# Zero products on TensorE in the waits of a fused Sinkhorn-attention and feed-forward kernel

## The chip, the cores and the metric

The kernel runs on one core of one Trainium2 chip. The metric is the device time of an execution in microseconds (us). The kernel before takes 242.38 us, the median of five runs that lie between 241.8 and 243.04.

TensorE (PE) multiplies matrices, VectorE (DVE) and ScalarE (ACT) do element-wise work and empty TensorE's accumulators in PSUM, GpSimd (POOL) issues most of the loads, and SyncE (SP) the stores and some small loads. Each engine works through its own list of instructions in order; semaphores make one wait for another.

## What is computed

Four batches of eight heads, 768 positions, head size 64. The positions are cut into 8 blocks of 96. A learned 8x8 matrix per head is normalised five times over rows and columns (Sinkhorn) and mixes the blocks of k and of v. Each block of q then attends to its own mixed block. The result, 3072 rows of 512, goes through a feed-forward layer of width 2048 with a squared ReLU.

```python
for _ in range(5):
    P = exp(P - max(P, axis=-1))
    P = P / (sum(P, axis=-1) + 1e-9);  P = P / (sum(P, axis=-2) + 1e-9)
k_sorted = einsum('bhij,bhjcd->bhicd', P, k_blocks)      # v_sorted in the same way
attn = softmax(q_block @ k_sorted_block.T / 8)           # block by block, 96 x 96
x = (attn @ v_sorted_block) as rows of 512
out = (s * relu(x @ w_in)**2 + b) @ w_out
```

## The kernel before

The work is cut into eight half-batches of 4 blocks x 96 = 384 rows, called t = 0 to 7 (t // 2 is the batch). One Python function emits each kind of piece, and the order in which the pieces are called is each engine's order of work; it is written out by hand from line 537 on. In the middle of the kernel `Queue` objects put attention pieces between feed-forward products. What the change touches lies before and in the first half-batch:

- `zt` (line 101) is a tile of zeros, and `warm_up(n)` (line 169) multiplies it by itself n times: 128x128 weights, 256 columns. Nothing reads the products.
- `q_half` (line 234) transposes half of q for batch 0; ScalarE copies the result to `qt`. Line numbers in the profile are those of the instruction: L244 for the transposes, L228 (VectorE) and L230 (ScalarE) for all copies out of PSUM, which go through `evac`.
- The Sinkhorn steps on `sn` (lines 187 to 201) alternate between ScalarE and VectorE.
- `build_pd1` calls `block_rows(0)`, whose product `pe` (L213) spreads the 8x8 matrices over 128 partitions; four VectorE instructions make the block matrix `pd1` from it (the last is L520).
- `k_piece` (L277) mixes the blocks of k with `pd1`, as product `tk`; the copies go to `ks`. `v_piece0` (L303) does it for v, 16 products of 64 columns per piece (`tv`), one copy each to `vs`. It reads its weights from `vb` with a stride of 64 elements.
- `s_piece` (L358) computes one pair of heads' scores for four blocks, and ScalarE takes their exp (L361, tile `at`).
- `p_piece` (L385) multiplies `at` by `vs` as `pv`. VectorE takes a reciprocal (L389) and writes the scaled values to `x` (L390). With `nn=2` it does only two of the four blocks, in one PSUM bank.
- `t_piece` (L413) transposes `x`; `ffn1` (L442) is the first feed-forward product, in eight slots of 8 products for two blocks or four.

Two pools of PSUM tiles matter. `psa` has three buffers of two banks (q transposes, the larger k pieces, v pieces, scores, feed-forward). `psb` has two buffers of one bank (zeros, `pe`, the smaller k pieces, the half-sized `p_piece` and `t_piece`). A tile can be taken again when everything that uses the earlier one in that buffer is done. In the kernel before, each zero product takes a new `psb` tile.

The loads that this part needs are issued on GpSimd's queue in this order: half of q, k and v of batch 0, the other half of q, then the weights, and later v, q and k of batch 1.

Of the kernel before, what the change touches and what calls it, by code (L numbers as in the profile page):

```python
# [9 lines left out]
FP = mybir.dt.float32  # L10
# [8 lines left out]
def kernel(  # L19
# [12 lines left out]
    nc = tc.nc  # L32
# [9 lines left out]
    HB = NB // 2  # L42
# [24 lines left out]
    psb = ctx.enter_context(tc.tile_pool(name="psb", bufs=2, space=bass.MemoryType.PSUM))  # L67
# [25 lines left out]
    def brows(b):  # L93
        return slice(b * 64, (b + 1) * 64), slice((b % 2) * 64, (b % 2) * 64 + 64)
# [6 lines left out]
    zt = const.tile([128, 256], BF)  # L101
# [41 lines left out]
    for c0 in range(0, d_ff, FCH):  # L143
        w = const.tile([128, NHP, FCH], BF, name=f"wi{c0}")
        nc.gpsimd.dma_start(
            out=w, in_=moe_w_in.rearrange("(hp p) f -> p hp f", p=128)[:, :, c0:c0 + FCH])
# [5 lines left out]
    for f0 in range(0, NF, FW):  # L152
        w = const.tile([128, FW, d_model], BF, name=f"wo{f0}")
        nc.gpsimd.dma_start(
            out=w, in_=moe_w_out.rearrange("(f p) n -> p f n", p=128)[:, f0:f0 + FW, :])
# [11 lines left out]
    ks = const.tile([128, 64, BLK], BF)  # L167

    def warm_up(n):
        for _ in range(n):  # L170
            wp = psb.tile([128, 256], FP, tag="b", name="wp")
            nc.tensor.matmul(out=wp, lhsT=zt[:, 0:128], rhs=zt, start=True, stop=True)  # L172

    def zero_pad(r0):
# [35 lines left out]
    def block_rows(g):  # L210

        pe = psb.tile([128, 512], FP, tag="b", name="pe")
        nc.tensor.matmul(out=pe[:, 0:NB * NB], lhsT=emat[:, g * 128:(g + 1) * 128],  # L213
                         rhs=sn.rearrange("p i j -> p (i j)"), start=True, stop=True)
        tmp = sk.tile([128, NB, NB], FP, name=f"tmp{g}")
        nc.vector.tensor_tensor(out=tmp, in0=pe[:, 0:NB * NB].rearrange("p (i j) -> p i j", j=NB),
                                in1=bcast(jsel, NB), op=ALU.mult)
        pt = sk.tile([128, NB], FP, name=f"pt{g}")
        nc.vector.tensor_reduce(out=pt, in_=tmp, axis=AX.X, op=ALU.add)
        return pt  # L220
# [5 lines left out]
    def evac(out, in_, eng):  # L226
        if eng == "v":
            nc.vector.tensor_copy(out=out, in_=in_)  # L228
        else:
            nc.scalar.copy(out=out, in_=in_)  # L230
# [3 lines left out]
    def q_half(half, eng):  # L234

        if half == 0:
            QT[0] = qtp.tile([128, NHP, S], BF, tag="qt", name="qt0")
        pr = slice(half * 64, half * 64 + 64)
        ps = psa.tile([128, 2, 1024], BF, tag="a", name="tq")
        for hp in range(NHP):  # L240
            for t in range(TQ):
                c0 = (hp % 2) * TG + t * 64
                for e in range(2):
                    nc.tensor.transpose(out=ps[e * 64:(e + 1) * 64, hp // 2, c0:c0 + 64],  # L244
                                        in_=qr[0][pr, 2 * hp + e, t, :], identity=ident[pr, pr])
        for a in range(2):
            evac(QT[0][:, 2 * a:2 * a + 2, half * TG:(half + 1) * TG].rearrange(
                     "q b (p t) -> q b p t", t=TQ),
                 ps[:, a, 0:2 * TG].rearrange("q (b t p) -> q b p t", b=2, t=TQ), eng)
# [15 lines left out]
    def k_piece(b, c0, nc2, nb, eng):  # L265

        pr = brows(b)[1] if nb == 1 else slice(0, 128)  # L270
        rhs = (pd1[pr] if b < 2 else pd2[pr, b - 2]).rearrange("p e m i -> p (e m i)")
        if nc2 * nb > 8:
            ps = psa.tile([128, nc2, nb * 64], FP, tag="a", name="tk")
        else:
            ps = psb.tile([128, nc2, nb * 64], FP, tag="b", name="tk")
        for c in range(nc2):
            nc.tensor.matmul(out=ps[:, c, :],  # L277
                             lhsT=kb[pr, c0 + 2 * c:c0 + 2 * c + 2, :].rearrange("p c d -> p (c d)"),
                             rhs=rhs, start=True, stop=True)
        g0 = (b % 2) * 32  # L280

        def half(cp):
            if b == 0:
                cs = slice(c0 + cp, c0 + 2 * nc2, 2)
            else:
                cs = slice(cp * (BLK // 2) + c0 // 2, cp * (BLK // 2) + c0 // 2 + nc2)
            for e in range(2):
                evac(ks[e * 64:(e + 1) * 64, g0:g0 + nb * 32, cs].rearrange(
                         "p (b g) c -> p b g c", b=nb),
                     ps[cp * 64:(cp + 1) * 64].rearrange(  # L290
                         "p c (b e g) -> p e b g c", b=nb, e=2)[:, e], eng)

        half(0)
        return lambda: half(1)

    def v_piece0(d0, n, eng):

        if n > 8:
            ps = psa.tile([128, n, 64], FP, tag="a", name="tv")
        else:  # L300
            ps = psb.tile([128, n, 64], FP, tag="b", name="tv")
        for t in range(n):
            nc.tensor.matmul(out=ps[:, t, :], lhsT=vb[0:64, :, d0 + t],  # L303
                             rhs=pd1[0:64].rearrange("p e m i -> p (e m i)"),
                             start=True, stop=True)
        evac(VS[0][:, :, d0:d0 + n], ps[0:BLK].rearrange("p t g -> p g t"), eng)
# [42 lines left out]
    def s_piece(t, hp):  # L349

        b, half = divmod(t, 2)
        g0 = (b % 2) * 32 + hp * NB + half * HB
        sc = psa.tile([BLK, 2, 512], FP, tag="a", name="sc")
        for n in range(HB):
            for e in range(2):
                pr = slice(e * 64, (e + 1) * 64)
                q0 = (half * HB + n) * BLK
                nc.tensor.matmul(out=sc[:, e, n * BLK:(n + 1) * BLK], lhsT=ks[pr, g0 + n, :],  # L358
                                 rhs=QT[b][pr, hp, q0:q0 + BLK], start=True, stop=True)
        at = atp.tile([BLK, 2, TG], BF, tag="at", name="at")  # L360
        nc.scalar.activation(out=at, in_=sc[:, :, 0:TG], func=AF.Exp, scale=scale)  # L361
        AT[t, hp] = at

    def p_piece(t, hp, n0=0, nn=HB):

        b, half = divmod(t, 2)
        at = AT[t, hp]
        if t not in X:
            X[t] = xp.tile([BLK, HB, d_model], BF, tag="x", name="x")
        x = X[t]  # L370
        atf = at.rearrange("p e t -> p (e t)")
        if nn < HB:
            p1 = psb.tile([128, 512], FP, tag="b", name="pv")
            pv = [p1[:, e * nn * VW:(e + 1) * nn * VW] for e in range(2)]
            pvv = p1[0:BLK, 0:2 * nn * VW].rearrange("p (e n w) -> p e n w", e=2, w=VW)
        else:
            p2 = psa.tile([128, 2, 512], FP, tag="a", name="pv")
            pv = [p2[:, 0], p2[:, 1]]
            pvv = p2[0:BLK, :, 0:nn * VW].rearrange("p e (n w) -> p e n w", w=VW)
        for e in range(2):  # L380
            for n in range(n0, n0 + nn):
                c0 = (e * HB + n) * BLK
                m = 128 if c0 + 128 <= 2 * TG else BLK
                gi = e * 32 + hp * NB + half * HB + n
                nc.tensor.matmul(out=pv[e][0:m, (n - n0) * VW:(n - n0 + 1) * VW],  # L385
                                 lhsT=atf[:, c0:c0 + m],
                                 rhs=VS[b][:, gi, :], start=True, stop=True)
        rec = rtp.tile([BLK, 2, HB], FP, tag="rec", name="rec")
        nc.vector.reciprocal(out=rec[:, :, 0:nn], in_=pvv[:, :, :, D])  # L389
        nc.vector.tensor_tensor(  # L390
            out=x[:, n0:n0 + nn, hp * 128:(hp + 1) * 128].rearrange("p n (e d) -> p e n d", e=2),
            in0=pvv[:, :, :, 0:D],
            in1=rec[:, :, 0:nn].unsqueeze(3).broadcast_to([BLK, 2, nn, D]), op=ALU.mult)
# [107 lines left out]
    def P2(t, hp):  # L501
        return lambda: (p_piece(t, hp), p_piece(t, hp + 1))
# [15 lines left out]
    def build_pd1():  # L518
        pt = block_rows(0)
        nc.vector.tensor_tensor(  # L520
            out=pd1, in0=hmask.rearrange("p (m e) i -> p e m i", e=2),
            in1=bass.AP(tensor=pt.tensor, offset=pt.offset,
                        ap=[list(pt.ap[0]), [0, 2], [0, NHP], list(pt.ap[1])]),
            op=ALU.mult)
# [10 lines left out]


    warm_up(38)
    q_half(0, "s")
    warm_up(12)
    build_pd1()  # L540
    k_piece(0, 0, 16, 1, "v")()
    k_piece(0, 32, 16, 1, "s")()
    k_piece(0, 64, 8, 1, "v")()
# [3 lines left out]
    v_piece0(32, 16, "v")  # L547
    s_piece(0, 0)
    s_piece(0, 1)
    v_piece0(48, 16, "v")  # L550
    s_piece(0, 2)
    s_piece(0, 3)
    q_half(1, "s")
    for hp in range(NHP):
        p_piece(0, hp, 0, 2)
    t_piece(0, "v", 0, 2)
    s_piece(1, 0)
    s_piece(1, 1)
# [4 lines left out]
    def P(t, hp, *r):  # L563
        return lambda: p_piece(t, hp, *r)
# [101 lines left out]
```

The softmax here doesn't subtract the row's maximum and nothing guards it: scores larger than these inputs give would overflow.

## Time and profile before

| what | value |
|---|---|
| median of five runs | 242.38 us (241.8 to 243.04) |
| profiled execution | 243.04 us |
| its span on the core | 241.3 us |
| mean granted clock of TensorE | 0.955 |
| PE busy in the span | 226.9 us, 94% |
| zero products (L172) | 50, 304 ns mean, 9.2 us busy |
| v products (L303) | 64, 271 ns mean, 6.0 us busy |

The profile is one execution, recorded by the hardware. Its span runs from the first to the last recorded instruction, and the execution took 1.74 us more than that. "Granted clock" is the share of full speed at which TensorE was let run. A product's duration contains its latency, and products overlap, so the distance between the starts of two of them is less than the duration. Each row names the line, the engine and the operation, with the output tile, an arrow and its inputs; "x16" means sixteen instructions merged into one row, and the brackets tell how long the engine stood idle before it and what ended that.

### The profile page before, as it was taken

The numbers are of one execution on the slowest core, as the hardware profiler recorded it, in microseconds if no ns is written. First come the engines' busy times: TensorE is split into PE (matmuls) and PEld (weight loads), VectorE is DVE, ScalarE is ACT, GpSimd is POOL, SyncE is SP. The second block draws the span as 40 slices with busy tenths as digits, with TensorE's granted clock in tenths as the row PEclk, the third lists the DMA queues.
The fourth block names the chain that finished last, engine by engine and source line by source line (L and its number), as shares of the span: only waits on it lengthen the run. The fifth ranks groups of instructions, "written<-read, shape, count | busy, mean of one in ns | idle before, by whom it ended". The sixth has DMA issues, their size and how long they took to land.

```text
span 241.3 us, 4882 instructions
## 1 busy us (share of the span) xinstructions
PE 226.9 (94%) x2059; PEld 135.9 (56%) x2080; DVE 134.1 (56%) x268; ACT 108.1 (45%) x154; POOL 39.4 (16%) x52
## 2 busy tenths in 40 slices
PE   8859799989999999999998999999999999999993
PEld 4558698855545555555554455666554556554441
DVE  5775547967993558766365748343353544342221
ACT  6356456435538541577726250656522225660000
POOL 7820000099960000460000000000000000000000
PEclk9975559999999999999999999999999999999999
DMA  4999999985999994599902061400014232001212
GB/s 59 183 196 211 220 200 206 229 211 95 136 158 173 273 307 104 117 114 105 161 11 87 3 152 46 109 0 3 1 47 125 69 109 47 0 3 43 79 51 87
DMA packets 29622, 27.33 MB, mean 113 GB/s; under 512 B 16928, under 2 KB 23840, under 8 KB 29088
## 3 DMA queue, kind: packets, MB, share of 16 engines
q0 software_dynamic: 8400, 15.21, 38.1%
q1 hardware_dynamic: 21200, 11.81, 20.8%
q8 instruction: 16, 0.26, 0.5%
q14 instruction: 6, 0.05, 0.1%
HBM read 29.63 MB, written 8.65 MB: 159 GB/s over the span
## 4 chain that ended last, share of the span: by engine, by line
PE 83%; DVE 7%; DMA 6%; issue 2%; POOL 1%; ACT 1%; POOLq 0%
PE hps L442 34%; PE ops L468 33%; DMA vb<-in_v_dram 6%; PE sc L358 3%; PE pv L385 3%; PE tv L303 2%; PE tk L277 2%; PE tq L259 2%; DVE x L390 2%; DVE ks L228 1%; PE tv L333 1%; DVE gt L447 1%; DVE vn L228 1%; DVE ot L459 1%; PE tq L244 1%
## 5 line engine op out<-in xcount | busy, mean ns | idle before, releaser
L442 PE MATMUL hps<-xt,wi 128*128 128x384 bf16 (+1 forms) x576 | 89.9, 314 | 1.0 <-DVE xt L228 1.0
L468 PE MATMUL ops<-wo,gt 128*128 128x512 bf16 x363 | 87.7, 379 | 1.5 <-issue 0.5
L446 ACT ACTIVATE rt<-hps 128x768 bf16<-128x768 f32 (+1 forms) x72 | 53.3, 740 | 53.8 <-PE hps L442 52.2
L442 PEld LDWEIGHTS <-wi 128*128 128x128 bf16 x576 | 54.7, 100 | 31.3 <-issue 2.3
L447 DVE TENSOR_TENSOR gt<-rt 128x768 bf16<-128x768 bf16 (+1 forms) x72 | 42.0, 586 | 42.3 <-ACT rt L446 41.8
L468 PEld LDWEIGHTS <-gt 128*128 128x128 bf16 x384 | 35.0, 98 | 38.4 <-issue 0.6
L361 ACT ACTIVATE at<-sc 96x768 bf16<-96x768 f32 x32 | 24.3, 802 | 35.2 <-PE sc L358 35.2
L459 DVE SCALAR_TENSOR_TENSOR ot<-ops,s_bc,bias 128x512 f32<-128x512 f32 x24 | 18.0, 749 | 38.0 <-PE ops L468 37.9
L390 DVE TENSOR_TENSOR x<-pv,rec 96x512 bf16<-96x512 f32 (+1 forms) x36 | 22.6, 628 | 1.3
L228 DVE CAST ks<-tk 64x512 bf16<-64x512 f32 (+1 forms) x36 | 20.8, 578 | 4.2 <-PE tk L277 3.7
L589 POOL TENSOR_TENSOR csum<-csum,wo 128x512 f32<-128x512 f32 x14 | 17.6, 1256 | 1.0
L230 ACT CAST ks<-tk 64x256 bf16<-64x256 f32 (+1 forms) x28 | 13.8, 491 | 8.0 <-PE tk L277 7.7
L385 PEld LDWEIGHTS <-at 96*128 96x128 bf16 (+1 forms) x256 | 12.4, 106 | 4.0 <-ACT qt L230 1.0
L385 PE MATMUL pv<-vs,at 96*128 96x66 bf16 (+1 forms) x256 | 13.2, 201 | 0.8 <-DVE rec L389 0.6
L358 PEld LDWEIGHTS <-ks 64*96 64x96 bf16 x256 | 8.4, 132 | 6.8 <-issue 5.0
L389 DVE RECIPROCAL rec<-pv 96x8 f32<-96x8 f32 (+1 forms) x36 | 6.9, 192 | 9.2 <-PE pv L385 9.2
L358 PE MATMUL sc<-qt,ks 64*96 64x96 bf16 x256 | 10.8, 224 | 1.0 <-DVE x L390 1.0
L172 PE MATMUL wp<-zt 128*128 128x256 bf16 x50 | 9.2, 304 | 1.1 <-DVE warm L104 1.1
L277 PEld LDWEIGHTS <-kb 64*128 64x128 bf16 x192 | 6.3, 95 | 5.4 <-issue 5.3
L277 PE MATMUL tk<-pd,kb 64*128 64x64 bf16 x192 | 7.8, 191 | 0.9 <-DVE pd L520 0.9
L303 PE MATMUL tv<-pd,vb 64*128 64x64 bf16 x64 | 6.0, 271 | 2.4 <-DMA vb<-in_v_dram 1.8
L230 ACT CAST vn<-tv 128x1024 bf16<-128x1024 f32 x6 | 6.1, 1012 | 4.1 <-DMA dv<-vn 3.4
(67 smaller groups left out, 101.0 us busy)
## 6 DMA issues: line engine op xcount, KB each, us to landing
out_dram<-ot SPq DMA_DIRECT2D x24, 256.0 KB, 2.2
kb<-in_k_dram POOLq DMA_DIRECT2D x4, 768.0 KB, 10.5
vb<-in_v_dram POOLq DMA_DIRECT2D x4, 768.0 KB, 18.9
qr<-in_q_dram POOLq DMA_DIRECT2D x3, 768.0 KB, 19.7
wi<-in_moe_w_in_dram POOLq DMA_DIRECT2D x2, 1024.0 KB, 18.8
wo<-in_moe_w_out_dram POOLq DMA_DIRECT2D x2, 1024.0 KB, 30.2
dv<-vn SPq DMA_DIRECT2D x6, 256.0 KB, 7.3
vs<-dv POOLq DMA_DIRECT2D x4, 384.0 KB, 11.6
```

The source lines that it names most:

```text
L228: nc.vector.tensor_copy(out=out, in_=in_)
L230: nc.scalar.copy(out=out, in_=in_)
L277: nc.tensor.matmul(out=ps[:, c, :], lhsT=kb[pr, c0 + 2 * c:c0 + 2 * c + 2, :].rearrange("p c d -> p (c d)"), rhs=rhs, start=True, stop=True)
L358: nc.tensor.matmul(out=sc[:, e, n * BLK:(n + 1) * BLK], lhsT=ks[pr, g0 + n, :], rhs=QT[b][pr, hp, q0:q0 + BLK], start=True, stop=True)
L361: nc.scalar.activation(out=at, in_=sc[:, :, 0:TG], func=AF.Exp, scale=scale)
L385: nc.tensor.matmul(out=pv[e][0:m, (n - n0) * VW:(n - n0 + 1) * VW], lhsT=atf[:, c0:c0 + m], rhs=VS[b][:, gi, :], start=True, stop=True)
L390: nc.vector.tensor_tensor(out=x[:, n0:n0 + nn, hp * 128:(hp + 1) * 128].rearrange("p n (e d) -> p e n d", e=2), in0=pvv[:, :, :, 0:D], in1 ...
L442: nc.tensor.matmul(out=hps[:, f, 0:nt], lhsT=wi_at(hp, f0 + f), rhs=xt_at(t, hp, n0, nn), start=(hp == 0), stop=(hp == NHP - 1))
L446: nc.scalar.activation(out=rt[:, :, 0:nt], in_=hps[:, :, 0:nt], func=AF.Relu)
L447: nc.vector.tensor_tensor(out=gt[:, f0:f0 + 2, c0:c0 + nt], in0=rt[:, :, 0:nt], in1=rt[:, :, 0:nt], op=ALU.mult)
L459: nc.vector.scalar_tensor_tensor(out=ot, in0=ops, scalar=s_bc, in1=bias, op0=ALU.mult, op1=ALU.add)
L468: nc.tensor.matmul(out=ops, lhsT=gt[:, f, m * 128:(m + 1) * 128], rhs=wo_at(f), start=(f == 0), stop=(f == NF - 1))
```

## The change

`warm_up` takes one PSUM tile per call instead of one per product. The second call has 20 products instead of 12. Three calls are new: 9 products behind `build_pd1` (so between `pe` and the first k piece in PE's order), 3 behind the first two score pieces, and 3 behind the next two. `p_piece` gets a parameter `zeros`; the four half-sized pieces of t = 0 that come first are given 2, and each then issues two products of zeros with 248 columns into the unused part of its own PSUM bank ahead of its own products. These are 31 zero products more, 81 in all. No load, copy or wait of another engine is added.

```diff
     def warm_up(n):
+        wp = psb.tile([128, 256], FP, tag="b", name="wp")
         for _ in range(n):
-            wp = psb.tile([128, 256], FP, tag="b", name="wp")
             nc.tensor.matmul(out=wp, lhsT=zt[:, 0:128], rhs=zt, start=True, stop=True)
...
-    def p_piece(t, hp, n0=0, nn=HB):
+    def p_piece(t, hp, n0=0, nn=HB, zeros=0):
...
             p1 = psb.tile([128, 512], FP, tag="b", name="pv")
             pv = [p1[:, e * nn * VW:(e + 1) * nn * VW] for e in range(2)]
+            for _ in range(zeros):
+                nc.tensor.matmul(out=p1[:, 264:512], lhsT=zt[:, 0:128], rhs=zt[:, 0:248],
+                                 start=True, stop=True)
...
     warm_up(38)
     q_half(0, "s")
-    warm_up(12)
+    warm_up(20)
     build_pd1()
+    warm_up(9)
     k_piece(0, 0, 16, 1, "v")()
...
     s_piece(0, 0)
     s_piece(0, 1)
+    warm_up(3)
     v_piece0(48, 16, "v")
     s_piece(0, 2)
     s_piece(0, 3)
+    warm_up(3)
     q_half(1, "s")
     for hp in range(NHP):
-        p_piece(0, hp, 0, 2)
+        p_piece(0, hp, 0, 2, 2)
     t_piece(0, "v", 0, 2)
```

## The prediction

> **What bounds the kernel now.** I read the page first. PE is busy for 226.9 of 241.3 us, and only one row of the page shows a stretch in which it is not at its best, the granted clock (one digit for 6.03 us of the span):
>
> ```profile
> PE 226.9 (94%) x2059; PEld 135.9 (56%) x2080; DVE 134.1 (56%) x268; ACT 108.1 (45%) x154; POOL 39.4 (16%) x52
> ...
> PE   8859799989999999999998999999999999999993
> ...
> PEclk9975559999999999999999999999999999999999
> ```
>
> The digits 7, 5, 5, 5 say that TensorE runs at about half speed from the third slice to the sixth. To place this I cut the span into equal stretches and read each one's busy time by engine and granted clock. The first time is the length, then busy time of PE and the other engines; the clock stands behind POOL:
>
> ```profile
> 8.07:11.48 3.41, 3.06 (x62) 1.90 (x60) 2.74 (x14) 1.58 (x4) 3.17 (x5) 1.00 1.05 216
> 11.48:14.89 3.41, 1.96 (x50) 1.82 (x50) 1.92 (x7) 0.73 (x2) 0.88 (x1) 1.00 0.94 197
> 14.89:18.31 3.42, 1.63 (x19) 1.66 (x20) 3.33 (x6) 3.35 (x6) 0.54 (x1) 0.50 1.18 200
> 18.31:21.72 3.41, 3.41 (x48) 3.37 (x48) 2.31 (x4) 2.21 (x5) 0.00 (x0) 0.50 1.13 213
> ...
> 28.55:31.96 3.41, 3.23 (x38) 2.68 (x37) 1.45 (x4) 1.50 (x2) 0.00 (x0) 0.50 0.93 174
> 31.96:35.37 3.41, 3.41 (x31) 3.19 (x30) 1.74 (x6) 1.20 (x3) 0.00 (x0) 0.50 1.24 208
> 35.37:38.79 3.42, 3.42 (x52) 3.16 (x50) 2.26 (x8) 2.33 (x5) 0.00 (x0) 1.00 1.25 207
> ```
>
> The clock drops at 14.89 us and returns at 35.37. The distance, 20.48 us, is six steps of 3.413, which is why I chose that grid: one step back from 14.89 three times is 4.65, where the products of zeros go from 421 to 269 ns each.
>
> Last, the chain of waits (start, us) and the order of time show what sets the pace in the slow stretch:
>
> ```profile
> 2.68 13.86 DMA vb<-in_v_dram
> ...
> 16.68 4.35 PE tv L303 x47
> 21.03 0.46 PE sc L358 x7
> ...
> 21.51 0.81 ACT at L361
> ...
> 22.36 1.38 PE tv L303 x14
> ...
> 23.96 1.23 DVE vs L228
> ...
> 25.23 1.49 PE tq L244 x39
> 26.72 0.35 PE pv L385 x4
> ```
>
> So the load of v fixes 16.54 us, whatever PE does before. Behind it PE at half clock, the exp and the eviction of v alternate until the first feed-forward slot at 30.61. From there on PE is nearly always busy, so what is won by then should last to the end.
>
> **Prices.** Eight feed-forward products of 192 columns take 1.47 us at half clock and 0.83 at full (order of time, 32.12 and 36.07). Less their last one's latency (0.37 and 0.27 from the durations), seven intervals give 157 and 80 ns, or 0.82 and 0.42 ns per column. A zero product of 256 columns is then 0.21 or 0.107 us, one of 248 columns 0.203 or 0.104. The row nearest in kind says more: the old 12 zeros take 2.02 us, (2.02 - 0.27)/11 = 0.159 each. But they take turns in two buffers, and (0.269 + 0.051)/2 = 0.160, a product's duration and the 51 ns of a semaphore instruction in the trace: each seems to wait for the last but one. With one tile per call I take 0.107, and keep 0.159 as the other end.
>
> **The change part by part.** *38 zeros, one tile.* About 16 run at half clock until 4.65 and 22 at 0.107, so they end near 7.1 instead of 8.2. The first quarter of q needs its load, issued at 1.33 and landed 6.1 us later (its shortest), 7.4 us. Nothing follows earlier: the copies of qt stand on ScalarE behind the fifth exp, which starts at 10.15. Price nothing.
>
> *20 for 12.* 20 x 0.107 = 2.1 us, from 8.4 at the earliest or 9.1 at the latest, so they end by 11.3; the broadcast product `pe` waits for `sn` until 12.02. Price nothing; at 0.159 they would end at 12.3, 0.3 late.
>
> *9 behind `pe`.* PE waits 0.90 us there for `pd1` (12.42 to 13.33), and from pe's own issue there is about 1.1. 9 x 0.107 = 0.96: nothing. At 0.159 it is 1.43, so k is some 0.5 late; queued behind are 48 k products and their evictions on VectorE and ScalarE. Even that is covered in the kernel before: VectorE ends the first v eviction at 20.12 and then idles 1.03 us for `tv`. If the cover is gone, 0.5 to 0.8 us is paid in full.
>
> *What they do to the clock.* Columns streamed in 11.48 to 14.89: 48 x 64 x 0.42 ns = 1.29 us, with `pe` at most 1.69, 38 to 50% of the window, and the clock drops at its end. Nine zeros make it 66 to 78%: it should stay. [...] PE was busy 1.96 of 3.41 us before the drop. [...] By the row, the next window streams less than the one that was punished: between 18 v products (at the old 91 ns pace) and 36 (half of it) of 27 ns, 14 to 28%, and the diff puts no zeros there. I go by the row: full clock until 18.31, then half.
>
> *v at full clock.* 48 products took 4.35 us, 91 ns each, where 64 columns at half clock are 53: the strided weight load may set this, and no strided load at full clock is in the trace. Bounds: 45 ns (all clock) and 91 (none). At 70 or less the third group is ready when VectorE is free at 20.12 instead of 21.15. I take the clock's end, because plain weight loads halve too (pv 186 to 95 ns). Step by step: eviction 20.12 to 21.34; scores from 20.15, exp from 20.8 to 21.6 (before 22.32); fourth group from 21.65 instead of 22.36. Gain 0.7; at the other end 0.
>
> *3 and 3 zeros.* At half clock 3 x 0.21 = 0.64 each. PE waits 0.58 before the fourth v group and 0.64 before `tq`; they fit, or cost 0.05 each. I count 0.
>
> *Two zeros before each first weighted value.* At half clock 0.41 each. The first is on the chain: 0.41. The second hides behind VectorE's work on x. The third waits for a buffer until x is done, then takes 0.05 + 0.41 + 0.38 = 0.84, against 0.58 that VectorE needs for the other x: 0.26. The fourth hides. Sum 0.67; at full clock about 0.2, since 0.56 fits in 0.58.
>
> *Return of the clock.* The windows 18.31 and 28.55 left it at half though PE was busy 3.41 and 3.23 us; 31.96, nearly all feed-forward, brought it back. So the columns count, not PE's busy time. By columns, 28.55 has about 2.9 us with its transposes (85%), 2.2 without. With 8 zeros (1.62 us), 16 pv (16 x 0.055 = 0.88) and 0.9 us of `tq`, the window from 25.13 gets to nearly all. [...] By the full count it returns at 28.55 and the gain is over 2 us, four slots of 1.53 us turning into 1.01 and more[...]. I take one window earlier, 31.96: 3.41 us hold 2.23 slots of 1.53, at full clock 2.23 x 1.01 = 2.25. Gain 1.16.
>
> **Sum**: - 0.70 + 0.67 - 1.16 = - 1.2 us. The profiled execution took 243.04 (span 241.3 and 1.74 around it), so 241.8 on its terms. It is the slowest of the five runs; [...] the difference goes to the median: 242.38 - 1.2 = **241.2**.
>
> **Rivals.** *The zeros cost and the clock gives nothing* (slower). The place is the chain through `pv`, 26.7 to 29.5, the price 0.67 plus 0.1 for the two threes, 243.15. It decides if v keeps its 91 ns pace or the drop comes before 16.7, and the return stays where it was. For it: 91 is well over 53, and that the zeros stand in PE's order before what is waited for. Should the zeros keep 0.159 and the v eviction lose its cover, it is 243.5 to 244. Against: the 1.03 us that VectorE idles for `tv`. *They cancel*: v gains 0.7, the zeros take 0.67, the return stays: 242.3. *The clock never drops*: v to scores as above, 0.9 us less; `tq` at 0.94 instead of 1.49, pv's zeros 0.2, `tr` at 0.51 for 0.89, a first slot near 28.5, so 2.1 there; then four slots at 1.01 for 1.53 to 1.0, some 1.3: 3.4 in all, 239.0. [...] against it the 57% window.
>
> **How the numbers follow.** A difference under 0.3% (0.73 us) can't be told from no change here. Chances: one window earlier or alike (1 to 3 us won) 0.38; never drops 0.12; cancel 0.22; slower 0.28. So faster 0.50, same 0.22, slower 0.28. The likeliest alone spans 239.5 to 241.5. The range to hold 8 in 10 cuts half of the never-drops case below and the dearest zeros above: 238.9 to 243.7.
>
> **What would show it.** The clock row still full past 14.9 and the drop a window later; zeros 0.107 apart; k evictions starting at 13.99 as before; v products under 70 ns apart and the third v eviction near 20.1; first feed-forward slot near 30.6; return at least 3 us before its old place. It is wrong if the drop stays near 15 us, if the v pace stays at 91 ns, or if the clock holds over the wait for v.

## The result, and the profile after

The changed kernel takes 243.57 us (median of 23 runs, 242.71 to 244.24), the kernel before 242.69 in the same set of runs (44 of them). The ratio is 1.0039, with a 95% interval of 1.0029 to 1.0050: about 0.9 us, 0.4%, slower. The forecast was 241.2 and faster. 243.57 also lies inside the range of 238.9 to 243.7, but only by a hair, and the direction was wrong; what happened is close to the rival "the zeros cost and the clock gives nothing", 0.77 us slower by its sum.

The clock row of the page after, and then the same stretches as before, on this execution's own grid of 3.413 us (length, busy time of PE, PEld, DVE, ACT and POOL, granted clock, DMA share, GB/s):

```profile
PEclk9995559999999999999999999999999999999998
```

```profile
11.67:15.08 3.41, 2.72 (x53) 2.32 (x54) 1.43 (x5) 0.20 (x2) 0.88 (x1) 1.00 0.91 187
15.08:18.50 3.42, 1.96 (x30) 1.87 (x27) 3.32 (x7) 3.36 (x5) 0.54 (x1) 1.00 1.21 207
18.50:21.91 3.41, 3.41 (x48) 3.33 (x47) 2.66 (x4) 2.50 (x6) 0.00 (x0) 0.50 1.13 211
21.91:25.32 3.41, 3.41 (x41) 2.71 (x38) 1.65 (x2) 1.93 (x3) 0.54 (x1) 0.50 1.12 213
25.32:28.74 3.42, 3.32 (x63) 2.54 (x62) 1.02 (x4) 2.39 (x4) 0.00 (x0) 0.50 1.20 239
28.74:32.15 3.41, 3.31 (x38) 2.50 (x38) 2.19 (x7) 0.47 (x1) 0.00 (x0) 0.50 0.98 182
32.15:35.56 3.41, 3.41 (x29) 3.20 (x28) 1.00 (x4) 2.02 (x4) 0.00 (x0) 0.50 1.25 208
35.56:38.98 3.42, 3.42 (x55) 3.21 (x53) 2.65 (x10) 2.27 (x5) 0.00 (x0) 1.00 1.24 207
```

The clock did what the forecast said of its drop: full through the stretch with the nine zeros, full through the next one, half from 18.50. It came back at 35.56, where the kernel before had it back at 35.37. The half speed lasted 17.06 us, five steps of 3.413, where the kernel before has six (20.48). So the hold was longer by one window, and nothing came back early, although PE was busy for nearly all of the three windows from 21.91 to 32.15 (3.41, 3.32 and 3.31 us).

What the longer hold bought is read from the v products. In steps of 1 us, the first column after the length is PE's busy time, with the number of products of which some part ran in the stretch; the clock stands next:

```profile
17.00:18.00 1.00, 1.00 (x13) 1.00 1.13 207
18.00:19.00 1.00, 1.00 (x14) 0.75 1.16 221
19.00:20.00 1.00, 1.00 (x14) 0.50 1.09 205
```

Thirteen or fourteen products run in a microsecond at full clock and fourteen at half (11 of them start in it each time): the v products do not go faster with the clock. Their 47 take 4.36 us here and took 4.35 before.

The chain of waits of the kernel after shows where time went instead (start and length in us):

```profile
16.89 4.36 PE tv L303 x47
21.25 0.75 PE sc L358 x16
21.99 0.76 PE wp L172 x3
22.75 1.38 PE tv L303 x14
...
24.98 0.76 PE wp L172 x3
25.73 1.42 PE tq L244 x26
27.15 0.53 PE pv L376 x2
27.68 0.23 PE pv L388 x4
...
28.63 0.59 PE pv L376 x2
29.22 0.23 PE pv L388 x4
...
30.17 0.98 PE tr L416 x8
```

Before, the exp and the eviction of v stood between these products; now the zeros (`wp`, and `pv` of L376) stand in their place, and they last longer than what they replaced. By the starts in the order of time, 5.79 us pass from the first v product to the fourth group instead of 5.68, from there to the q transposes 2.98 instead of 2.87, and from those to the transposes of x 4.51 instead of 3.75. That is 0.11 + 0.11 + 0.76 = 0.98 us, all at half clock. The first feed-forward slot starts at 31.89 instead of 30.61; besides these 0.98 us, v's load landed 0.21 later in this execution, and 0.09 lies in the stretch from the transposes to the slot. By the fifth slot (36.83 instead of 36.07) the lag is 0.76: the clock's return came at almost the same moment, so fewer slots ran before it at half speed. The span is 0.8 us longer.

### The profile page after: what moved, and what is told of

Same layout as the page of the kernel before. It is cut to its first block, busy times and chain, and to the rows that moved or that the text cites. A ratio compares the mean times of both kernels' runs of the same rounds, so it can differ in the third digit from the quotient of the medians.

```text
span 242.1 us, 4942 instructions
## 1 busy us (share of the span) xinstructions
PE 229.9 (95%) x2090; PEld 139.4 (58%) x2111; DVE 134.2 (55%) x268; ACT 108.0 (45%) x154; POOL 39.4 (16%) x52
## 4 chain that ended last, share of the span: by engine, by line
PE 85%; DMA 6%; DVE 5%; issue 2%; POOL 1%; ACT 0%; POOLq 0%
PE hps L445 34%; PE ops L471 34%; DMA vb<-in_v_dram 6%; PE sc L358 4%; PE pv L388 3%; PE tv L303 2%; PE tk L277 2%; PE tq L259 2%; DVE x L393 1%; PE tv L333 1%; DVE gt L450 1%; DVE vn L228 1%; PE wp L172 1%; DVE ot L462 1%; DVE ks L228 1%
## 5 line engine op out<-in xcount | busy, mean ns | idle before, releaser
L388 PEld LDWEIGHTS <-at 96*128 96x128 bf16 (+1 forms) x256 | 12.9, 106 | 3.3
L388 PE MATMUL pv<-vs,at 96*128 96x66 bf16 (+1 forms) x256 | 13.3, 201 | 0.1
L172 PE MATMUL wp<-zt 128*128 128x256 bf16 x73 | 11.3, 319 | 1.1 <-DVE warm L104 1.1
L172 PEld LDWEIGHTS <-zt 128*128 128x128 bf16 x73 | 7.8, 113 | 3.1 <-DVE warm L104 1.1
```

## The experiments

Two theories stood at first. A: the zeros on the chain are the whole loss, and the clock held over v is worth nothing. B: the loss comes from the fills ahead of v, by a delay of k or a shifted return of the clock.

**e1: only the zeros ahead of the first weighted values.**

```diff
     for hp in range(NHP):
-        p_piece(0, hp, 0, 2)
+        p_piece(0, hp, 0, 2, 2)
```

(with the two products of 248 columns in `p_piece`; everything else as before)

> The kernel before with one part of the change alone: the two zero products ahead of each of the four first weighted values. Theory A (the zeros on the chain are the whole loss): the first slot of the feed-forward comes 0.7 to 0.8 us later and the kernel is 0.5 to 0.8 us slower than before. Theory B (the loss lies in the fills ahead of v, which delay k or move the clock's return): no difference, within 0.2 us.

Measured: 1.0040 (1.0025 to 1.0054), 0.6 to 1.3 us slower, as much as the whole change. In order of time (start, duration):

```profile
25.16 1.49 PE L244 MATMUL tq<-ident,qr 64*64 64x64 bf16 x48 [0.64 <-DVE vs L228]
26.58 0.60 PE L376 MATMUL pv<-zt 128*128 128x248 bf16 x2
26.97 0.43 PE L388 MATMUL pv<-vs,at 96*128 96x66 bf16 x4
...
28.12 0.59 PE L376 MATMUL pv<-zt 128*128 128x248 bf16 x2
28.51 0.43 PE L388 MATMUL pv<-vs,at 96*128 96x66 bf16 x4
...
29.66 0.98 PE L416 MATMUL tr<-ident,x 96*128 96x96 bf16 x8
```

From the q transposes to those of x 4.50 us pass, against 3.75 in the kernel before. The zeros of the first piece push its products from 1.42 to 1.81 us behind the start of `tq`, and those of the third delay it again: before, its products started 2.65 us behind `tq`, now its zeros start at 2.96 and its products at 3.35. In the changed kernel's chain these zeros start 0.05 us behind the end of the first piece's `x` (28.58 and 28.63): they waited for its buffer. The clock is back at about 34.6 us here (0.71 on average from 34 to 35), and by an estimate it fell while k ran, between 13.3 and 15.3 us: its 48 products take 2.06 us instead of 1.56. That leaves some 20 us at half speed, as in the kernel before (20.48). Theory A holds, B falls.

**e2: the change without those zeros.**

```diff
     for hp in range(NHP):
-        p_piece(0, hp, 0, 2, 2)
+        p_piece(0, hp, 0, 2)
```

> The changed kernel without the zero products in the first weighted values; all its other zeros stay. Theory A: 0.1 to 0.3 us slower than before, which is what the two groups of three cost. Theory B: as slow as the changed kernel, 0.8 to 1.0 us over the kernel before.

Measured: 1.0011 (0.9997 to 1.0025). No difference that is clear, and the middle, 0.3 us, is what the two groups of three cost in the trace of the changed kernel (0.22).

**e3: only the fills ahead of k** (one tile per call, 20 for 12, and the 9).

```diff
     s_piece(0, 1)
-    warm_up(3)
...
     s_piece(0, 3)
-    warm_up(3)
...
     for hp in range(NHP):
-        p_piece(0, hp, 0, 2, 2)
+        p_piece(0, hp, 0, 2)
```

(against the changed kernel)

> Only one tile per call, 20 for 12 and the 9 zeros; neither the threes nor those in the weighted values. The clock should hold beyond the start of the v products. Theory A: no difference to before within 0.1 us, since the v products stay 91 ns apart at full clock, and so a longer hold buys nothing. Theory C (the forecast's v step): 0.5 to 0.7 us faster. Theory B: 0.3 us slower or more.

Measured: 0.9989 (0.9973 to 1.0006), again no clear difference. The interval reaches from 0.65 us faster to 0.15 slower, so the times alone don't quite rule out theory C; the trace does. The clock held until 18.6 us in its profile (0.82 on average from 18 to 19, 0.50 after), and v to feed-forward took its old time:

```profile
12.58 1.16 PE L172 MATMUL wp<-zt 128*128 128x256 bf16 x9
13.86 1.57 PE L277 MATMUL tk<-pd,kb 64*128 64x64 bf16 x48
16.87 4.39 PE L303 MATMUL tv<-pd,vb 64*128 64x64 bf16 x48 [1.44 <-DMA vb<-in_v_dram]
...
30.75 1.46 PE L445 MATMUL hps<-xt,wi 128*128 128x192 bf16 x8
```

16.87 to 30.75 is 13.88 us; before it was 13.93 (16.68 to 30.61). So the fills ahead of k cost nothing that shows, as the forecast had it, and are worth nothing there, as it had not.

**e4 and e5: what sets the 91 ns of a v product.** The weights of a v product lie 64 elements apart. In e4 (on the kernel before) and e5 (on the changed one) they are neighbours; the products then use other numbers than v's rows, so only their pace is asked.

```diff
-            nc.tensor.matmul(out=ps[:, t, :], lhsT=vb[0:64, :, d0 + t],
+            nc.tensor.matmul(out=ps[:, t, :],
+                             lhsT=vb[0:64].rearrange("p c d -> p (c d)")[:, (d0 + t) * 128:(d0 + t + 1) * 128],
```

> The kernel before with the same neighbouring weights in the v products, mostly at half clock (the output is wrong in the same way). If the strided load sets the 91 ns: 53 to 60 ns apart at half clock. If not: still 91 ns.

> The changed kernel with the v products reading their weights as 128 neighbouring elements instead of with a stride of 64 (other numbers than v's rows, so the output is wrong; the time of the products is what is asked). If the strided load sets the 91 ns: 27 to 35 ns apart while the clock is full. If not: still 91 ns.

The v products of e4, at half clock:

```profile
16.81 3.01 PE L303 MATMUL tv<-pd,vb 64*128 64x64 bf16 x48 [1.46 <-DMA vb<-in_v_dram]
```

and two groups of e5, at full clock by their pace:

```profile
17.99 1.09 PE L303 MATMUL tv<-pd,vb 64*128 64x64 bf16 x32 [0.61 <-ACT ks L230]
```

Less the last product's latency (0.27 and 0.19), that is 2.74/47 = 58 ns at half clock and 0.90/31 = 29 at full, where the 48 k products ahead of them, in 1.57 us, come (1.57 - 0.19)/47 = 29 ns apart too. With the stride they come 91 ns apart at half clock, and 11 start in a microsecond at full clock as at half in the changed kernel. So the strided load sets the 91 ns, and in these traces that limit does not follow the clock. The kernels took 241.64 and 242.25 us in one run each, too few to compare: with v no longer bound by its loads, the scores wait for the copies on ScalarE (1.74 us in e5).

**h1: the clock held over v, first attempt.** If the weight load takes 91 ns, there is time for more columns: 64 at full clock are 27 ns of it, 192 are 80. Each v product gets its block matrix up to three times, 192 columns; the surplus lands where the next products of the piece write their own values afterwards. 14 zeros fill the wait for v.

```diff
         for t in range(n):
-            nc.tensor.matmul(out=ps[:, t, :], lhsT=vb[0:64, :, d0 + t],
-                             rhs=pd1[0:64].rearrange("p e m i -> p (e m i)"),
+            kk = min(3, 8 - t % 8)
+            src = pd1[0:64].rearrange("p e m i -> p (e m i)")
+            nc.tensor.matmul(out=ps[:, t:t + kk, :], lhsT=vb[0:64, :, d0 + t],
+                             rhs=bass.AP(tensor=src.tensor, offset=src.offset,
+                                         ap=[list(src.ap[0]), [0, kk], [1, 64]]),
...
+    warm_up(14)
     v_piece0(0, 16, "v")
...
-    warm_up(3)
+    warm_up(6)
...
-    warm_up(3)
+    warm_up(9)
```

> The changed kernel with the clock meant to be held over v too: 14 zeros in the wait for v, each v product with up to 192 instead of 64 columns (the same block matrix repeated; the extra columns land where the next products write), 6 and 9 zeros in place of the threes. If the v products are bound by their weight load, the wider ones still come about 91 ns apart at full clock, the array stays busy, and the clock holds to the feed-forward: 1.5 to 3 us faster than before. If width is paid for, the v step is 1 to 3 us longer and the kernel slower.

Measured: 1.0207 (1.0174 to 1.0240), 5 us slower. The mean clock was 0.992, and it held over v to the feed-forward: 46 wide v products took 4.47 us and each of the first slots 0.82 or 0.83. But PE had no product from 15.34 to 19.70, and the 14 zeros behind that took 2.96 us, about 0.2 each, the pace of half clock. One row of the waits tells why (us in total, times, longest):

```profile
PE wp L172 <- ACT ks L230: 4.4, 1, 4.4
```

The zeros took a PSUM buffer that ScalarE was still emptying of k. All of v stood behind them in PE's order and started at 22.59 instead of 16.7.

**h2 and h3: the same without that wait.** The 13 zeros go into the first v piece's own tile. h2 has 4 and 4 zeros for the threes and none in the weighted values; h3 has 4 and 6, and the change's two in each weighted value. (The diff leaves out the wider v products, which are those of h1.)

```diff
-    def v_piece0(d0, n, eng):
+    def v_piece0(d0, n, eng, zeros=0):
...
+        for _ in range(zeros):
+            nc.tensor.matmul(out=ps[:, 0:4, :].rearrange("p t g -> p (t g)"), lhsT=zt[:, 0:128], rhs=zt,
+                             start=True, stop=True)
...
-    v_piece0(0, 16, "v")
+    v_piece0(0, 16, "v", 13)
```

> As the run before it with wider v products, but the 13 zeros in the wait for v are written into the first v piece's own PSUM tile, so that they wait for no copy of k; 4 zeros in place of each group of three, none before the weighted values. If the clock's hold up to the feed-forward is what pays (theory A: four slots at 1.0 instead of 1.5 us, and nothing gained before them): 1.2 to 2.5 us faster than before. If the clock drops again between the scores and the feed-forward: within 0.5 us of before.

> The same with 4 and 6 zeros and with the two zeros ahead of each first weighted value as in the change. Theory A: at full clock these cost 0.2 us or less, so 1 to 2.3 us faster than before, and at most 0.4 slower than the run without them where that one holds the clock.

Measured: h2 0.9924 (0.9886 to 0.9962), h3 0.9923 (0.9887 to 0.9960): both about 1.9 us faster than the kernel before, and alike. The four runs of h2 fall into two pairs, 240.2 us at a mean clock of 1.00 and 241.5 at 0.993; the profile is of one at 1.00, and only there the clock is shown to hold throughout. The clock row of h2, and its order of time:

```profile
PEclk9999999999999999999999999999999999999999
```

```profile
16.85 4.47 PE L308 MATMUL tv<-pd,vb 64*128 64x192 bf16 x46
...
29.78 0.82 PE L451 MATMUL hps<-xt,wi 128*128 128x192 bf16 x8 [0.25 <-DVE xt L228]
...
33.23 0.83 PE L451 MATMUL hps<-xt,wi 128*128 128x192 bf16 x8
```

46 products of mostly 192 columns take 4.47 us, about 94 ns each, 3 more than with 64 columns: the added columns fit into the load's time. From the first v product to the fourth group 5.69 us pass, against 5.68 before: even at full clock throughout, v gains nothing. From the first v product to the feed-forward it is 12.93 us instead of 13.93, and the first four slots (29.78 to 33.23) take 3.45 instead of 5.46. Most of the clock's worth lies in these slots, not in v. The zeros of the weighted values run at full clock in h3 (two take 0.38 or 0.39 us instead of 0.60) and cost less there: 4.90 us from the q transposes to the first slot against 4.55 in h2, 0.35 us that the times don't resolve.

**g1 and g2: which part holds the clock.** g1 is h2 with the old 64 columns (the diff is against h2); g2 is the kernel before with the wider products of h1 and no zeros added.

```diff
-            nc.tensor.matmul(out=ps[:, t:t + kk, :], lhsT=vb[0:64, :, d0 + t],
+            nc.tensor.matmul(out=ps[:, t, :], lhsT=vb[0:64, :, d0 + t],
...
```

> The run that held the clock (13 zeros in the wait for v, 4 and 4 later, none before the weighted values), but with the v products at their old 64 columns. Theory A2 (the v products themselves let the clock drop, 27 ns of columns in 91): the clock drops between 18 and 22 us and is half until the feed-forward, 0 to 0.5 us slower than before. Theory D (the 1.7 us wait for v drops it): it holds as in the other, 1.5 to 2.2 us faster.

> The kernel before with the wider v products alone, no zeros added or moved. The clock drops near 15 us as before. Theory A2: at half clock 192 columns take 159 ns instead of 91, so the v step is 2 to 3.5 us longer until the clock is back after a full window of it, near 21 to 24 us; then the feed-forward starts at full clock and takes back 1.5 to 2 us: 0 to 2 us slower in all. If the wide products alone hold the clock: 1.5 to 2.2 us faster.

Measured: g1 1.0038 (1.0016 to 1.0060), g2 1.0134 (1.0118 to 1.0150). Two windows from the v products on, first of g1:

```profile
17.84:21.25 3.41, 3.41 (x52) 3.41 (x52) 2.66 (x5) 2.78 (x5) 0.00 (x0) 1.00 1.12 212
21.25:24.66 3.41, 3.41 (x46) 2.79 (x41) 1.58 (x2) 1.58 (x3) 0.17 (x1) 0.50 1.12 212
```

The same two stretches of h2:

```profile
17.84:21.25 3.41, 3.41 (x43) 3.41 (x42) 2.58 (x4) 2.82 (x5) 0.00 (x0) 1.00 1.13 213
21.25:24.66 3.41, 3.23 (x57) 2.96 (x55) 1.72 (x2) 1.80 (x3) 0.23 (x1) 1.00 1.12 212
```

PE is busy for the whole first stretch in both. In g1 the clock drops at its end (0.60 on average from 21.2 to 21.4), in h2 it stays, and the two differ in the width of the v products alone. Filling the wait for v only moved the drop, from 18.50 in the changed kernel to 21.25; with narrow v products it still came. g1 loses somewhat more than expected, since its fours run at half clock: 0.17 us more than before ahead of the fourth v group and 0.34 ahead of the q transposes. In its profile v starts at 16.69 right behind the 13 zeros (15.16 and 1.59 us) with no wait between them, and in e2 v could start at 15.98: the wait that they fill is not as long in every run. g2 shows the reverse, at half clock throughout:

```profile
19.55:22.97 3.42, 3.42 (x26) 3.42 (x25) 0.75 (x1) 1.03 (x1) 0.00 (x0) 0.50 1.12 211
```

46 products take 6.77 us here, some 142 ns each, so the scores start 2.3 us later after v's arrival, and the clock doesn't come back in this window, although by an estimate columns stream nearly all the time (168 on average at 0.84 ns are 141 of the 142 ns). The return was expected near 21 to 24 us; it came at 36.6, in the feed-forward, so nothing was taken back and the loss is 3.2 us instead of 0 to 2. The weights of these products are 64 x 128, those of the feed-forward 128 x 128.

**t1 and t2: do transposes count?** The first 38 zero products are replaced by 80 transposes of zeros (t1) or 80 ordinary products with the identity (t2), 128x128 each.

```diff
-    warm_up(38)
+    wt = psb.tile([128, 1024], BF, tag="b", name="wt")
+    for _ in range(80):
+        nc.tensor.transpose(out=wt[:, 0:128], in_=zt[:, 0:128], identity=ident)
```

> The kernel before with its 38 first zero products replaced by 80 transposes of 128x128 zeros, back to back from the cold start. If transposes don't count for the clock: the later ones are as far apart as the first ones, about 107 ns, through all 80 (8.5 us). If they count: the distance halves to about 55 ns after 3.4 to 6.8 us.

> The control: 80 ordinary products of zeros with the identity, 128 columns, in the same place. The distance falls from about 107 to about 55 ns after 3.4 to 6.8 us, whichever holds for transposes.

The products that run in a microsecond, in t1:

```profile
6.00:7.00 1.00, 1.00 (x12) 1.00 0.41 53
...
9.00:10.00 1.00, 1.00 (x22) 1.00 1.03 209
```

and t2:

```profile
6.00:7.00 1.00, 1.00 (x12) 1.00 0.45 57
...
9.00:10.00 1.00, 1.00 (x22) 1.00 0.97 197
```

Both start at 4.55 us and nearly double their pace near 8 us, from 12 or 13 a microsecond (up to 14 from 7 to 8 us) to 22. That is 3 to 3.5 us after the start; the 3.4 to 6.8 us expected are one to two steps of the forecast's grid of 3.413. Transposes bring the clock up here just as products do. (The clock column shows 1.00 before and after the change of pace, so the pace is read here.)

## Why the prediction was wrong, step by step

- *38 zeros; 20 for 12; 9 behind `pe`*: right. The 20 end at 10.5 (8.14 + 2.36) with 1.53 us to spare; the nine fit. (8.14 to 10.50, less the last one's 0.269, over 19 intervals is 0.110 us, as taken for one tile per call.) k starts when its load lands, 0.52 us later than before (13.85 instead of 13.33), and that is covered. e3 shows no cost.
- *What they do to the clock*: right in what happened. By the row, full until 18.3; it was 18.50. The case "never drops" was the author's estimate, for which no trace spoke, and was rightly kept small. The measure, columns alone, was not the right one (see the return of the clock).
- *v at full clock*: **this step failed.** It had both ends, 45 and 91 ns, and took the clock's, "because plain weight loads halve too" (186 to 95 ns for pv). The load here is not plain, and the row itself was at 91. Gain 0 instead of 0.7: e5 shows that the strided load sets the pace (29 ns without the stride), and the traces of the changed kernel, e3 and h2 that v is no faster with more of it at full clock (4.36 us for 47 products, 4.39 for 48, 4.47 for 46 wide ones; before, 4.35 for 47). The nearest row should have decided.
- *3 and 3 zeros*: counted as 0, or 0.05 each; they cost 0.11 each. From the first zero of a group to the product behind it 0.75 us pass (21.93 to 22.68, 24.91 to 25.66), where 3 x 0.21 = 0.64 was taken. Why a group takes longer than its columns stays open.
- *Two zeros before each first weighted value*: right, 0.67 forecast, 0.76 measured, and at the two places named; 0.42 of it at the first piece (its reciprocal starts 2.28 us behind `tq`, before 1.86).
- *Return of the clock*: **this step failed too.** It took the columns as the measure and expected the denser stretch to bring the clock back one window earlier, 1.16 us; that it was one window, and not the two of the full count, was the author's estimate. The return didn't come early in the changed kernel or in e1: 0 instead of 1.16. The dense stretch was there, with PE busy for 3.32 of 3.42 us from 25.32 and, by columns, more than the window's length (1.22 times), and the clock stayed at half. So columns alone are not the measure. Leaving out the transposes, as in the forecast's other count (2.2 us), would not explain it either: in t1 transposes brought the clock up, from 12 to 22 a microsecond. What the prediction left out may be the size of a product's weights. In g2 products with weights of 64 x 128 filled 99% of a window by columns (about 24 of 168 columns at 0.84 ns in 3.42 us) and left the clock at half. By columns times the size of the weights, an estimate from the traces that the last section explains, the two windows from 25.32 and 28.74 come to 62% and 68% in the changed kernel (37% and 69% from 25.13 and 28.55 before), and the windows at whose end the clock came back to 95% and 94%. This was found by comparing the windows afterwards; no run was made to isolate it.

With the terms as measured, 0 + 0.76 + 0.22 - 0 = 1.0 us slower, against 0.9 measured.

## What to carry to other kernels

Work that only keeps the clock up can be free in a wait at full speed (the nine zeros behind `pe`, e3), and costs about double at half speed (0.76 us in the change, 0.35 at full speed in h3, for the same eight products); place it where the clock is certain to be full, and not in front of something that others wait for. Look also at the buffer it takes (h1) and at whether the wait is there in every run (g1). Before counting on a faster clock, ask which products would become faster: the v products with their strided weights didn't (91 ns at both clocks). Widening them was the better filler here, because with narrow ones the clock was still lost (h2 against g1: 0.9924 and 1.0038); but at half clock the width is paid for (g2: 142 ns instead of 91).

## What was not expected of the hardware

- A product of 64 x 128 weights read with a stride of 128 bytes comes every 91 ns at half clock (the kernel before) and, at 11 in a microsecond, at full clock too (the changed kernel), against 58 and 29 with neighbouring weights (e4, e5).
- With the same products, 192 columns instead of 64 cost about 3 ns each at full clock (94 in h2 against 91), and 51 at half (142 in g2).
- The length of the half speed shows in the times. In the 42 runs of the kernel before beside e1, 18 have a mean granted clock of 0.964 or 0.965 and a median of 241.9 us; 24 have 0.954 to 0.958 and 242.7. From the groups' median clocks, 0.964 and 0.955, and a span of 241 us, the second ran by an estimate some 4 us more at half speed.
- By columns times the size of the weights, the full clock was kept in a window with 39%, and half clock stayed in one with 69%. These are estimates: each product's columns, at 0.42 ns at full clock and twice that at half, times the rows and columns of its weights as a share of 128 x 128, the largest in the traces, added up in a window and divided by its 3.41 us. The windows are those of the views above and of the prediction, with the one from 25.13 that it names; h2, which has no change of clock, has g1's stretch.

| run and window (us) | clock in it, then | PE busy | columns alone | columns x size of the weights |
|---|---|---|---|---|
| after, 11.67:15.08 | full, full | 0.80 | 0.63 | 0.45 |
| h2, 17.84:21.25 | full, full | 1.00 | 0.79 | 0.39 |
| before, 11.48:14.89 | full, half | 0.57 | 0.39 | 0.19 |
| g1, 17.84:21.25 | full, half | 1.00 | 0.44 | 0.20 |
| after, 15.08:18.50 | full, half | 0.57 | 0.19 | 0.10 |
| before, 25.13:28.55 | half, half | 0.75 | 1.00 | 0.37 |
| g2, 19.55:22.97 | half, half | 1.00 | 0.99 | 0.50 |
| after, 25.32:28.74 | half, half | 0.97 | 1.22 | 0.62 |
| after, 28.74:32.15 | half, half | 0.97 | 0.99 | 0.68 |
| before, 28.55:31.96 | half, half | 0.95 | 0.99 | 0.69 |
| before, 31.96:35.37 | half, full | 1.00 | 0.99 | 0.94 |
| after, 32.15:35.56 | half, full | 1.00 | 0.99 | 0.95 |

PE's busy share overlaps between windows that end differently, and so do columns alone at half clock; the last column doesn't. "Columns alone" passes 1 because some products share the time: the 48 `tq` of 64 columns come 27 ns apart at half clock, half of the 54 that their columns would take. No threshold follows from so few windows, and that the size of the weights is the cause is inferred from the fit; no run shows it by itself.
